# State space part in pairs of chunks with gram products as row tiles, and PReLU split between two engines

## The chip, the cores and the metric

One core of a Trainium2 chip runs the kernel: TensorE (matrix products, from SBUF into PSUM), VectorE, ScalarE, GpSimd, and SyncE, whose queue issues all of the kernel's DMAs. The metric is the device time of one execution in microseconds. All data are float32.

## The reference, cut to what matters

A selective state space layer (4 batches, 8 heads, 768 tokens, head size 32, state size 16), then a feed-forward block with PReLU on its 3072 rows of 256 values. The reference takes chunks of 32 tokens; the result doesn't depend on the size of a chunk.

```python
for c in range(nc):                       # chunks of tokens, state carried along
    cum = np.cumsum(log(clip(a))[chunk])
    L = np.exp(cum_i - cum_j) * causal    # decay from token j to token i
    M = einsum('bhin,bhjn->bhij', C, B) * L
    y = einsum('bhij,bhjd->bhid', M, x) + einsum('bhin,bhnd->bhid', C, state) * exp(cum)
    state = exp(sum(la)) * state + sum_j(B_j x_j * exp(cum_last - cum_j))
h = y_as_rows @ w_in                      # (3072, 256) by (256, 2048)
g = np.maximum(h, 0) + alpha * np.minimum(h, 0)
out = g @ w_out                           # (2048, 256)
```

## The kernel before

Chunks have Q = 128 tokens, so there are 24, six to a batch. Per batch, `batch_prep` brings B and C into layout with (head, state) on partitions by transposes on TensorE (`transposed`, L186, copied out at L190 on ScalarE and L192 on VectorE), scans a into running products `pf` (forward, L207) and `pr` (backward, L209), and makes `cd` = C times `pf`, `br` = B times `pr`, and `bn`, which is `br` transposed back.

Per chunk, `chunk` does the following. GpSimd clamps `abc`, a copy of a on all partitions (L239). VectorE scans it into the decay matrices `dec` of the eight heads (L243). ScalarE makes `cz`, eight copies of C in each of which only one head's rows are kept (L249). TensorE multiplies `bh` with four heads of `cz` at a time, 512 columns and all 128 rows of the array (`gram`, L254); VectorE multiplies by `dec` (`m`, L256). TensorE adds the part of the state (L262) and the eight products of `m` and `xt` (L267), as tiles of 32 columns of the array, into `y`; ScalarE copies `y` into `xT` (L273). The next state is `dps` (L278), masked to the blocks of the heads (L281, L284), plus the decayed old one (L285).

The second part takes groups of four chunks, 512 tokens. `hidden` makes 16 tiles `hp` of 128 x 512 (L299), each by two products; PReLU is two operations of VectorE, `neg` = min(hp, 0) * alpha (L302) and `gt` = max(hp, 0) + neg (L304). `output` multiplies `gt` with `w_out` (`po`, L315), copies to `o_sb` (L317) and stores. In the trace each float32 product is two instructions of TensorE.

The weights come as float64 and are made float32 by seven operations of VectorE and one of GpSimd for each of 32 pieces (L141 to L154): those of `w_in` after the first chunks, those of `w_out` during the first group. The code of a group emits, for each of four quarters, one chunk of the next group and then four tiles of `hidden`; `output` follows. The Tile framework orders each engine's instructions from that by priority and readiness as it models them; on the chip each engine runs its own in the order so fixed. PSUM has eight banks: two for `gram`, one for `y`, one for all other products of the state space part (`sm`), two for `hp`, two for `po`.

Of the kernel before, what the change touches and what calls it, by code (L numbers as in the profile page):

```python
# [18 lines left out]
def kernel(  # L19
# [27 lines left out]
    HD = H * D  # L47
    d_model, d_ff = moe_w_in.shape
# [4 lines left out]
    NG = NCH // GC  # L53
    FQ = 4
# [5 lines left out]
    ld = ctx.enter_context(tc.tile_pool(name="ld", bufs=1))  # L60
# [17 lines left out]
    loads = {}  # L78

    def load_batch(b):  # L80
        bc = ld.tile([P, 2, H, R * N], F32, name="bc")
        for i, src in enumerate((B, C)):
            nc.sync.dma_start(out=bc[:, i], in_=src[b].rearrange("h (p r) n -> p h (r n)", r=R))
        ahn = ld.tile([P, S], F32, name="ahn")
        for h in range(H):
            row = a[b, h : h + 1, :]
            nc.sync.dma_start(
                out=ahn[h * N : (h + 1) * N, :],
                in_=bass.AP(tensor=row.tensor, offset=row.offset, ap=[[0, N], [1, S]]),
            )  # L90
        loads["b", b] = bc, ahn

    def load_chunk(gc):
        b, c = divmod(gc, CPB)
        sl = slice(c * Q, (c + 1) * Q)
        first = a[b, 0:1, sl]
        abc = lda.tile([P, H * Q], F32, name="abc")
        nc.sync.dma_start(
            out=abc.rearrange("p (h t) -> p h t", h=H),
            in_=bass.AP(tensor=first.tensor, offset=first.offset, ap=[[0, P], [S, H], [1, Q]]),  # L100
        )
        xt = ldx.tile([P, HD], F32, name="xt")
        nc.sync.dma_start(
            out=xt.rearrange("p (h d) -> p h d", h=H), in_=x[b, :, sl, :].rearrange("h p d -> p h d")
        )
        loads["c", gc] = abc, xt

    load_batch(0)
    for gc in range(2):
        load_chunk(gc)  # L110
# [28 lines left out]
        # the upper word without its sign orders as a float32: hold it to the  # L139
        # words whose exponent float32 has, with its zero and its infinity  # L140
# [41 lines left out]
    def transposed(dst, src, eng):  # L182
        for r0 in range(0, R, 3):
            ps = ps_s.tile([P, 512], F32, name="sm")
            for r in range(3):
                nc.tensor.transpose(ps[:, r * P : (r + 1) * P], src(r0 + r), ident)  # L186
            o = dst(r0)
            i = ps[:, : 3 * P].rearrange("q (r p) -> q r p", r=3)
            if eng == "act":
                nc.scalar.copy(out=o, in_=i)  # L190
            else:
                nc.vector.tensor_copy(out=o, in_=i)  # L192

    def batch_prep(b):
        """B and C with (h n) on partitions; the running product of a from each
        chunk's start up to a token (pf), and from after it to the chunk's end (pr)."""
        bc, ahn = loads.pop(("b", b))
        d0 = prep.tile([P, S + 1], F32, name="d0")
        d1 = prep.tile([P, S], F32, name="d1")
        nc.vector.tensor_scalar(out=d0[:, :S], in0=ahn, scalar1=1e-6, scalar2=1.0,  # L200
                                op0=ALU.max, op1=ALU.min)
        nc.gpsimd.memset(d1, 0.0)
        nc.vector.tensor_copy(out=d1[:, ::Q], in_=d0[:, 0:S:Q])
        nc.vector.memset(d0[:, ::Q], 0.0)
        pf = bat.tile([P, S], F32, name="pf")
        pr = prep.tile([P, S], F32, name="pr")
        nc.vector.tensor_tensor_scan(out=pf, data0=d0[:, :S], data1=d1, initial=0.0,  # L207
                                     op0=ALU.mult, op1=ALU.add)
        nc.vector.tensor_tensor_scan(out=pr[:, ::-1], data0=d0[:, 1:][:, ::-1],  # L209
                                     data1=ends[:, ::-1], initial=0.0,  # L210
                                     op0=ALU.mult, op1=ALU.add)

        bh = bat.tile([P, S], F32, name="bh")
        ch = bat.tile([P, S], F32, name="ch")
        for i, t, eng in ((0, bh, "act"), (1, ch, "dve")):
            # token p * R + r of the batch is row p of piece r
            src = bc[:, i].rearrange("p h (r n) -> p r h n", r=R)
            nat = prep.tile([P, R, H * N], F32, name="nat")
            nc.scalar.copy(out=nat.rearrange("p r (h n) -> p r h n", h=H), in_=src)
            tv = t.rearrange("q (p r) -> q r p", r=R)  # L220
            transposed(lambda r0: tv[:, r0 : r0 + 3], lambda r: nat[:, r], eng)
        cd = bat.tile([P, S], F32, name="cd")
        nc.vector.tensor_tensor(out=cd, in0=ch, in1=pf, op=ALU.mult)
        br = prep.tile([P, S], F32, name="br")
        nc.vector.tensor_tensor(out=br, in0=bh, in1=pr, op=ALU.mult)
        bn = bat.tile([P, CPB, P], F32, name="bn")
        transposed(lambda r0: bn[:, r0 : r0 + 3], lambda c: br[:, c * Q : (c + 1) * Q], "act")
        pre[b] = pf, bh, ch, cd, bn

    def chunk(gc):  # L230
        b, c = divmod(gc, CPB)
        if c == 0:
            batch_prep(b)
        pf, bh, ch, cd, bn = pre[b]
        abc, xt = loads.pop(("c", gc))
        sl = slice(c * Q, (c + 1) * Q)
# [4 lines left out]
        nc.gpsimd.memset(abc[:, ::Q], 0.0)  # L241
        dec = work.tile([P, H, Q], F32, name="dec")
        nc.vector.tensor_tensor_scan(out=dec.rearrange("p h t -> p (h t)"), data0=abc,  # L243
                                     data1=ident_h, initial=0.0, op0=ALU.mult, op1=ALU.add)

        # C with all rows but a head's own cleared, head by head
        cz = work.tile([P, H, Q], F32, name="cz")
        for h in range(H):
            nc.scalar.mul(cz[:, h], ch[:, sl], bm3[:, h, 0:1])  # L249
        m = work.tile([P, H, Q], F32, name="m")  # L250
# [24 lines left out]
        if c < CPB - 1:  # L275
# [6 lines left out]
            else:  # L282
# [91 lines left out]
```

## Time and profile before

| what | value |
|---|---|
| median of 3 runs | 524.29 us (523.46 to 526.51) |
| span of the profiled execution | 523.9 us |
| TensorE products busy | 453.4 us, 87% |
| VectorE busy | 340.6 us, 65% |
| ScalarE busy | 85.6 us, 16% |
| GpSimd busy | 70.9 us, 14% |
| moved by DMA | 32.31 MB |

The profiled execution's own time is known as its span, from the first to the last instruction; the runs give device times. Busy times are unions over the span and say nothing yet of which engine set the end in which stage.

### The profile page before, as it was taken

The numbers are of one execution on the slowest core, as the hardware profiler recorded it, in microseconds if no ns is written. First come the engines' busy times: TensorE is split into PE (matmuls) and PEld (weight loads), VectorE is DVE, ScalarE is ACT, GpSimd is POOL, SyncE is SP. The second block draws the span as 40 slices with busy tenths as digits, with TensorE's granted clock in tenths as the row PEclk, the third lists the DMA queues.
The fourth block names the chain that finished last, engine by engine and source line by source line (L and its number), as shares of the span: only waits on it lengthen the run. The fifth ranks groups of instructions, "written<-read, shape, count | busy, mean of one in ns | idle before, by whom it ended". The sixth has DMA issues, their size and how long they took to land. (4 is left out here: it accounts for less than half of the span.)

```text
span 523.9 us, 4981 instructions
## 1 busy us (share of the span) xinstructions
PE 453.4 (87%) x1825; PEld 270.0 (52%) x1825; DVE 340.6 (65%) x587; ACT 85.6 (16%) x249; POOL 70.9 (14%) x93
## 2 busy tenths in 40 slices
PE   0285656595989999998999999998999999999997
PEld 0142222352447644685434786443884447863586
DVE  3889999999898599403899404879107964038600
ACT  2174220006220010001732000054002200000000
POOL 3413443222324000000010000102000000000000
PEclk9997967987999999999899999999999999999999
DMA  8734646323225012102222102204000000000000
GB/s 188 198 103 131 154 127 175 111 72 98 53 67 137 27 50 60 41 21 60 55 68 61 39 21 62 60 0 102 0 20 22 0 1 0 21 20 0 1 20 20
DMA packets 67192, 32.31 MB, mean 62 GB/s; under 512 B 34896, under 2 KB 62560, under 8 KB 67168
## 3 DMA queue, kind: packets, MB, share of 16 engines
q1 hardware_dynamic: 67168, 32.00, 23.0%
q8 instruction: 14, 0.23, 0.2%
q14 instruction: 10, 0.08, 0.0%
HBM read 28.84 MB, written 3.15 MB: 61 GB/s over the span
## 5 line engine op out<-in xcount | busy, mean ns | idle before, releaser
L299 PE MATMUL hp<-xT,w_in 128*128 128x512 f32 x384 | 186.4, 625 | 12.0 <-DVE gt L304 11.9
L315 PE MATMUL po<-w_out,gt 128*128 128x256 f32 x768 | 169.4, 380 | 3.8 <-POOL abc L241 2.7
L315 PEld LDWEIGHTS po<-w_out,gt 128*128 128x128 f32 x768 | 145.3, 190 | 30.7 <-issue 5.8
L299 PEld LDWEIGHTS hp<-xT,w_in 128*128 128x128 f32 x384 | 70.3, 197 | 97.5 <-issue 57.3
L317 DVE COPY o_sb<-po 128x256 f32<-128x256 f32 x24 | 10.1, 422 | 130.5 <-PE po L315 130.4
L302 DVE TENSOR_SCALAR neg<-hp,alpha 128x512 f32<-128x512 f32 x96 | 71.5, 746 | 25.1 <-PE hp L299 24.9
L249 ACT ACTIVATE cz<-ch,bmask 128x128 f32<-128x128 f32 x192 | 59.3, 390 | 99.3 <-PE gram L254 85.5
L304 DVE SCALAR_TENSOR_TENSOR gt<-hp,neg 128x512 f32<-128x512 f32 x96 | 66.0, 689 | 2.4
L239 POOL TENSOR_SCALAR abc<-abc 128x1024 f32<-128x1024 f32 x24 | 35.7, 1488 | 223.4 <-DMA abc<-in_a_dram 196.9
L243 DVE TENSOR_TENSOR_SCAN dec<-abc,ident_h 128x1024 f32<-128x1024 f32 x24 | 55.3, 2304 | 1.9 <-POOL abc L241 1.4
L254 PE MATMUL gram<-cz,bh 128*128 128x512 f32 x96 | 54.2, 669 | 1.3 <-ACT cz L249 1.2
L273 ACT COPY xT<-y 128x256 f32<-128x256 f32 x24 | 8.9, 372 | 160.9 <-PE y L267 160.8
L256 DVE TENSOR_TENSOR m<-gram,dec 128x512 f32<-128x512 f32 x48 | 31.9, 682 | 4.7 <-PE gram L254 4.6
L267 PE MATMUL y<-m,xt 128*32 128x128 f32 x384 | 21.4, 301 | 12.7 <-DVE m L256 12.7
L267 PEld LDWEIGHTS y<-m,xt 128*32 128x32 f32 x384 | 8.2, 112 | 39.0 <-DVE m L256 20.7
L254 PEld LDWEIGHTS gram<-cz,bh 128*128 128x128 f32 x96 | 18.0, 206 | 18.0 <-issue 12.5
L186 PE MATMUL sm<-ident,nat 128*128 128x128 f32 x48 | 11.1, 353 | 12.6 <-DVE alpha L175 3.9
L154 POOL TENSOR_TENSOR w_out<-wr,wt 128x256 uint32<-128x256 uint32 x16 | 15.4, 960 | 34.0 <-DVE wr L150 22.6
L186 PEld LDWEIGHTS sm<-ident,nat 128*128 128x128 f32 x48 | 6.6, 172 | 21.6 <-DVE ch L192 5.3
L262 PEld LDWEIGHTS y<-cd,state 128*128 128x128 f32 x80 | 12.3, 198 | 9.5 <-issue 8.5
L190 ACT COPY bh<-sm 128x384 f32<-128x384 f32 x8 | 6.8, 845 | 61.0 <-PE sm L186 61.0
L154 POOL TENSOR_TENSOR w_in<-wr,wt 128x256 uint32<-128x256 uint32 x16 | 12.7, 797 | 28.9 <-DVE wr L150 28.7
(43 smaller groups left out, 200.0 us busy)
## 6 DMA issues: line engine op xcount, KB each, us to landing
abc<-in_a_dram SPq DMA_DIRECT2D x24, 512.0 KB, 4.0
raw<-in_moe_w_in_dram SPq DMA_DIRECT2D x16, 256.0 KB, 2.9
raw<-in_moe_w_out_dram SPq DMA_DIRECT2D x16, 256.0 KB, 2.7
xt<-in_x_dram SPq DMA_DIRECT2D x24, 128.0 KB, 2.7
out_dram<-o_sb SPq DMA_DIRECT2D x12, 256.0 KB, 2.1
bc<-in_B_dram SPq DMA_DIRECT2D x4, 384.0 KB, 3.6
bc<-in_C_dram SPq DMA_DIRECT2D x4, 384.0 KB, 4.9
ahn<-in_a_dram SPq DMA_DIRECT2D x32, 48.0 KB, 3.1
```

Of the source, the lines that this page charges most:

```text
L154: nc.gpsimd.tensor_tensor(out=d, in0=r, in1=t, op=ALU.add)
L186: nc.tensor.transpose(ps[:, r * P : (r + 1) * P], src(r0 + r), ident)
L239: nc.gpsimd.tensor_scalar(out=abc, in0=abc, scalar1=1.0, scalar2=1e-6, op0=ALU.min, op1=ALU.max)
L243: nc.vector.tensor_tensor_scan(out=dec.rearrange("p h t -> p (h t)"), data0=abc, data1=ident_h, initial=0.0, op0=ALU.mult, op1=ALU.add)
L249: nc.scalar.mul(cz[:, h], ch[:, sl], bm3[:, h, 0:1])
L254: nc.tensor.matmul(gram.rearrange("p h t -> p (h t)"), bh[:, sl], cz[:, hs].rearrange("p h t -> p (h t)"), start=True, stop=True)
L256: nc.vector.tensor_tensor(out=m[:, hs], in0=gram, in1=dec[:, hs], op=ALU.mult)
L267: nc.tensor.matmul(y[32 * k : 32 * k + 32, w], xt[:, h * D : (h + 1) * D], m[:, h], start=(c == 0 and w == 0), stop=True, tile_position=(0 ...
L299: nc.tensor.matmul(hp, w_in[:, k, f * P : (f + 1) * P], xts[g][:, k], start=(k == 0), stop=(k == KC - 1))
L302: nc.vector.tensor_scalar(out=neg, in0=hp, scalar1=0.0, scalar2=alpha[:, f : f + 1], op0=ALU.min, op1=ALU.mult)
L304: nc.vector.scalar_tensor_tensor(out=gt[:, j], in0=hp, scalar=0.0, in1=neg, op0=ALU.max, op1=ALU.add)
L315: nc.tensor.matmul(po[:, :d_model], gts[g, f // FQ][:, f % FQ, ts], w_out[:, f], start=(f == 0), stop=(f == NF - 1))
```

## The change

The state space part runs in pairs of chunks, 12 in all. B and C are loaded per pair in their natural layout (`nat`: tokens on partitions), in rows of 16 values, and transposed per pair (four transposes, `tp`). `bn` is no longer transposed back: GpSimd multiplies the natural B by the backward running product, which is made from 96 rows (batch, head, chunk) twice in the run (`rows_prep`) and transposed. `cz` becomes two masked copies of C, even and odd heads (mask `par`), and `gram` becomes, per chunk, four products on 32 rows of the array each (two heads, 256 columns), into four PSUM banks. `m` is then made in four operations per pair. The masked product `dm` and the copy into `xT` are made for both chunks at once. The pools `ps_g` and `ps_y` go; all state space products share four banks (`ss`). The copy of a for the batch (`ahn`) is one DMA. PReLU becomes relu(hp) and relu(-hp) on ScalarE and one operation of VectorE, relu(hp) - alpha * relu(-hp). Comments are also taken out.

```diff
-    ps_g = ...(name="ps_g", bufs=2)   # also ps_y bufs=1, ps_s bufs=1
+    ps_s = ...(name="ps_s", bufs=4)
+    def load_pair(gp):
+        b, c = divmod(2 * gp, CPB)
+        nat = ldx.tile([P, 2, 2, H * N], F32, name="nat")
+        abc = lda.tile([P, 2, H * Q], F32, name="abc")
+        xt = ldx.tile([P, 2, HD], F32, name="xt")
+        for k in range(2):
+            sl = slice((c + k) * Q, (c + k + 1) * Q)
+            for i, src in enumerate((B, C)):
+                nc.sync.dma_start(out=nat[:, i, k].rearrange("p (h n) -> p h n", h=H),
+                                  in_=src[b, :, sl, :].rearrange("h p n -> p h n"))
...
+    def rows_prep(i):
+        rows = loads.pop(("r", i))
+        d0 = prep.tile([RW, Q + 1], F32, name="r0")
+        nc.vector.tensor_scalar(out=d0[:, :Q], in0=rows, scalar1=1e-6, scalar2=1.0,
+                                op0=ALU.max, op1=ALU.min)
...
+        nc.vector.tensor_tensor_scan(out=pr[:, ::-1], data0=d0[:, 1:][:, ::-1],
+                                     data1=ends[:RW, ::-1], initial=0.0,
+                                     op0=ALU.mult, op1=ALU.add)
+        ps = ps_s.tile([P, 512], F32, name="ss")
+        nc.tensor.transpose(ps[:, :RW], pr, ident[:RW, :RW])
...
+        for k in range(2):
+            nc.vector.tensor_tensor_scan(out=dec[:, k].rearrange("p h t -> p (h t)"),
+                                         data0=abc[:, k], data1=ident_h, initial=0.0,
+                                         op0=ALU.mult, op1=ALU.add)
+        tp = ps_s.tile([P, 512], F32, name="ss")
+        for i in range(2):
+            for k in range(2):
+                nc.tensor.transpose(tp[:, (2 * i + k) * P : (2 * i + k + 1) * P], nat[:, i, k],
+                                    ident)
+        ct = tp[:, 2 * P :]
+        bh = work.tile([P, 2, Q], F32, name="bh")
+        nc.scalar.copy(out=bh.rearrange("p k t -> p (k t)"), in_=tp[:, : 2 * P])
+        cz = work.tile([P, 2, 2, Q], F32, name="cz")
+        for e in range(2):
+            nc.scalar.mul(cz[:, e].rearrange("p k t -> p (k t)"), ct, par[:, e : e + 1])
+        cd = work.tile([P, 2, Q], F32, name="cd")
+        nc.vector.tensor_tensor(out=cd.rearrange("p k t -> p (k t)"), in0=ct,
+                                in1=pf[:, c * Q : (c + 2) * Q], op=ALU.mult)
...
-        for h in range(H):
-            nc.scalar.mul(cz[:, h], ch[:, sl], bm3[:, h, 0:1])
-        for g in range(2):
-            hs = slice(4 * g, 4 * g + 4)
-            gram = ps_g.tile([P, 4, Q], F32, name="gram")
-            nc.tensor.matmul(gram.rearrange("p h t -> p (h t)"), bh[:, sl],
-                             cz[:, hs].rearrange("p h t -> p (h t)"), start=True, stop=True)
-            nc.vector.tensor_tensor(out=m[:, hs], in0=gram, in1=dec[:, hs], op=ALU.mult)
+        gram = [ps_s.tile([P, 2, 2 * Q], F32, name="ss") for r in range(4)]
+        for k in range(2):
+            for r in range(4):
+                rs = slice(32 * r, 32 * r + 32)
+                nc.tensor.matmul(gram[r][:, k], bh[rs, k], cz[rs, :, k], start=True, stop=True,
+                                 tile_position=(32 * r, 0), skip_group_check=True)
+        for r in range(4):
+            hs = slice(2 * r, 2 * r + 2)
+            nc.vector.tensor_tensor(out=m[:, :, hs].rearrange("p k h t -> p k (h t)"), in0=gram[r],
+                                    in1=dec[:, :, hs].rearrange("p k h t -> p k (h t)"),
+                                    op=ALU.mult)
...
             neg = op.tile([P, GT], F32, name="neg")
-            nc.vector.tensor_scalar(out=neg, in0=hp, scalar1=0.0, scalar2=alpha[:, f : f + 1],
-                                    op0=ALU.min, op1=ALU.mult)
-            nc.vector.scalar_tensor_tensor(out=gt[:, j], in0=hp, scalar=0.0, in1=neg,
-                                           op0=ALU.max, op1=ALU.add)
+            nc.scalar.activation(out=gt[:, j], in_=hp, func=ACTF.Relu)
+            nc.scalar.activation(out=neg, in_=hp, func=ACTF.Relu, scale=-1.0)
+            nc.vector.scalar_tensor_tensor(out=gt[:, j], in0=neg, scalar=nalpha[:, f : f + 1],
+                                           in1=gt[:, j], op0=ALU.mult, op1=ALU.add)
...
-            if g + 1 < NG:
-                ssm((g + 1) * GC + q)
+            if g + 1 < NG and q % 2 == 0:
+                ssm((g + 1) * GC // 2 + q // 2)
```

The pair's order in the code is: clamp and `dec`, transposes, `bh`, `cz`, `cd`, then `bn`, `dps`, `dm` and the states, then `gram` and `m`, then all of `y`, then the copy into `xT`. The loads of a pair are issued one pair ahead.

## Rows read from the trace of the kernel before

**Rows 1.** The page, busy time of each engine.
```profile
PE 453.4 (87%) x1825; PEld 270.0 (52%) x1825; DVE 340.6 (65%) x587; ACT 85.6 (16%) x249; POOL 70.9 (14%) x93
```
**Rows 2.** Windows: length, busy PE, PEld, DVE, ACT, POOL; clock; DMA share, GB/s.
```profile
0.00:19.20 19.20, 0.26 (x1) 0.18 (x1) 10.24 (x10) 3.71 (x10) 6.97 (x15) 1.00 0.77 182
19.20:161.30 142.10, 101.14 (x391) 49.79 (x392) 134.43 (x313) 37.90 (x109) 46.30 (x50) 0.86 0.41 112
161.30:520.30 359.00, 351.99 (x1435) 220.07 (x1434) 195.54 (x267) 43.98 (x130) 17.66 (x29) 1.00 0.13 35
```
**Rows 3.** Waits of PE, 161.3 to 520.3 us: total, times, longest.
```profile
PE hp L299 <- DVE gt L304: 3.9, 5, 1.2
PE sm L186 <- DVE ch L192: 2.3, 2, 2.0
PE y L267 <- DVE m L256: 0.4, 1, 0.4
```
**Rows 4.** The chain that ended last: start, us, what, instructions.
```profile
341.03 0.34 PE sm L186 x3
...
405.29 1.72 PE gram L254 x4
407.00 0.44 PE y L262 x4
...
407.88 0.36 PE y L267 x8
408.24 1.05 PE hp L299 x2
...
429.77 0.57 PE y L267 x16
...
436.67 27.63 PE po L315 x128
464.30 28.31 PE hp L299 x64
```
**Rows 5.** Groups of DVE by shape, 0 to 161.3 us: busy us, mean ns.
```profile
L243 DVE TENSOR_TENSOR_SCAN dec<-abc,ident_h 128x1024 f32<-128x1024 f32 x10 | 23.3, 2331 | 1.0 <-POOL abc L241 1.0
...
L302 DVE TENSOR_SCALAR neg<-hp,alpha 128x512 f32<-128x512 f32 x16 | 11.8, 740 | 2.5 <-PE hp L299 2.5
L304 DVE SCALAR_TENSOR_TENSOR gt<-hp,neg 128x512 f32<-128x512 f32 x16 | 10.8, 680 | 0.0
...
L209 DVE TENSOR_TENSOR_SCAN pr<-d,ends 128x768 f32<-128x768 f32 x2 | 4.3, 2172 | 0.0
...
L192 DVE COPY ch<-sm 128x384 f32<-128x384 f32 x4 | 3.3, 834 | 0.4 <-PE sm L186 0.4
...
L223 DVE TENSOR_TENSOR cd<-ch,pf 128x768 f32<-128x768 f32 x2 | 2.4, 1180 | 0.0
L225 DVE TENSOR_TENSOR br<-bh,pr 128x768 f32<-128x768 f32 x2 | 1.9, 952 | 0.7 <-ACT bh L190 0.7
```
**Rows 6.** Groups of ACT by shape, whole span.
```profile
L249 ACT ACTIVATE cz<-ch,bmask 128x128 f32<-128x128 f32 x192 | 59.3, 390 | 99.3 <-PE gram L254 85.5 <-DVE ch L192 13.8
...
L273 ACT COPY xT<-y 128x256 f32<-128x256 f32 x24 | 8.9, 372 | 160.9 <-PE y L267 160.8
...
L190 ACT COPY bh<-sm 128x384 f32<-128x384 f32 x8 | 6.8, 845 | 61.0 <-PE sm L186 61.0
...
L190 ACT COPY bn<-sm 128x384 f32<-128x384 f32 x8 | 3.8, 474 | 4.5 <-PE sm L186 4.4
```
**Rows 7.** Timeline of the first stage: start, us, instruction, idle before it.
```profile
11.16 2.60 DVE L209 TENSOR_TENSOR_SCAN pr<-d,ends 128x768 f32<-128x768 f32 x1
...
66.11 0.43 PE L267 MATMUL y<-m,xt 128*32 128x128 f32 x8 [2.12 <-DVE m L256]
```
**Rows 8.** Groups of PE by shape, 161.3 to 520.3 us: gram.
```profile
L254 PE MATMUL gram<-cz,bh 128*128 128x512 f32 x60 | 29.0, 597 | 0.0
```
**Rows 9.** DMA queues: packets, MB, share of 16 engines' span.
```profile
q1 hardware_dynamic: 67168, 32.00, 23.0%
```

More of the change, by code (lines that the diff above doesn't have):

```diff
@@ L47 @@
     HD = H * D
+    RW = batch // 2 * H * CPB
     d_model, d_ff = moe_w_in.shape
@@ L53 @@
     NG = NCH // GC
+    NP = NCH // 2
     FQ = 4
@@ new lines, in load_batch, with load_rows @@
+        loads["b", b] = ahn
+    def load_rows(i):
+        rows = ld.tile([RW, Q], F32, name="rows")
+        nc.sync.dma_start(out=rows, in_=a.rearrange("b h (c t) -> (b h c) t", t=Q)[i * RW : (i + 1) * RW])
+        loads["r", i] = rows
+    def load_pair(gp):
[8 more added lines that the diff above has]
+                                  in_=src[b, :, sl, :].rearrange("h p n -> p h n"))
+            first = a[b, 0:1, sl]
@@ L87, in load_batch @@
             nc.sync.dma_start(
-                out=ahn[h * N : (h + 1) * N, :],
-                in_=bass.AP(tensor=row.tensor, offset=row.offset, ap=[[0, N], [1, S]]),
-            )
[L91 to L106, printed above, removed]
+                out=abc[:, k].rearrange("p (h t) -> p h t", h=H),
@@ L108 @@
+                in_=bass.AP(tensor=first.tensor, offset=first.offset, ap=[[0, P], [S, H], [1, Q]]),
+            )
+            nc.sync.dma_start(out=xt[:, k].rearrange("p (h d) -> p h d", h=H),
+                              in_=x[b, :, sl, :].rearrange("h p d -> p h d"))
+        loads["p", gp] = nat, abc, xt
+    load_rows(0)
     load_batch(0)
-    for gc in range(2):
-        load_chunk(gc)
+    load_pair(0)
     w_in = const.tile([P, KC, d_ff], F32, name="w_in")
@@ L180 @@
     state = {}
[L182 to L192, printed above, removed]
+    prt = {}
@@ L213, in batch_prep @@
[L213 to L231, printed above, removed]
+        pre[b] = pf
+    def pair(gp):
+        b, c = divmod(2 * gp, CPB)
@@ L232, in chunk @@
         if c == 0:
             batch_prep(b)
-        pf, bh, ch, cd, bn = pre[b]
-        abc, xt = loads.pop(("c", gc))
-        sl = slice(c * Q, (c + 1) * Q)
+        pf = pre[b]
+        nat, abc, xt = loads.pop(("p", gp))
+        last = c + 2 == CPB
         nc.gpsimd.tensor_scalar(out=abc, in0=abc, scalar1=1.0, scalar2=1e-6,
                                 op0=ALU.min, op1=ALU.max)
[L241 to L244, printed above, removed]
@@ new lines, in pair @@
+        bn = work.tile([P, 2, H * N], F32, name="bn")
+        i, bi = divmod(b, 2)
+        pj = prt[i].rearrange("p (b h c) -> p b c h", b=2, h=H)[:, bi, c : c + 2]
+        nc.gpsimd.tensor_tensor(
+            out=bn.rearrange("p k (h n) -> p k h n", h=H),
+            in0=nat[:, 0].rearrange("p k (h n) -> p k h n", h=H),
+            in1=pj.unsqueeze(3).to_broadcast([P, 2, H, N]), op=ALU.mult)
+        nk = 1 if last else 2
+        dps = ps_s.tile([P, 512], F32, name="ss")
+        for k in range(nk):
+            nc.tensor.matmul(dps[:, k * HD : (k + 1) * HD], bn[:, k], xt[:, k], start=True, stop=True)
@@ new lines, in pair @@
+        dm = work.tile([P, 2, HD], F32, name="dm")
+        nc.vector.tensor_tensor(
+            out=dm[:, :nk], in0=dps[:, : nk * HD].rearrange("p (k m) -> p k m", m=HD),
+            in1=bmask.unsqueeze(1).to_broadcast([P, nk, HD]), op=ALU.mult)
+        st = [state.get(b)]
+        for k in range(nk):
+            if st[k] is None:
+                st.append(dm[:, k])
+                continue
+            new = work.tile([P, HD], F32, name=f"state{k}")
+            e = (c + k + 1) * Q - 1
+            nc.vector.scalar_tensor_tensor(out=new, in0=st[k], scalar=pf[:, e : e + 1],
+                                           in1=dm[:, k], op0=ALU.mult, op1=ALU.add)
+            st.append(new)
@@ L331, in weights @@
             load_weights(*p)
-    for i in range(GC):
+    for i in range(GC // 2):
         ssm(i)
-        weights(in_pieces, i, GC)
+        weights(in_pieces, i, GC // 2)
     for g in range(NG):
```

116 lines of the change are left out of this document (59 added, 57 removed).

## The prediction

> **What bounds the kernel now.** I read the busy line of the page first [rows 1]: TensorE is busy 87% of 523.9 us, VectorE 65%, ScalarE 16%. An average hides the stages, so next came the windows [rows 2]. The reader is to see two regimes in them. From 19.2 to 161.3 us VectorE is busy 134.4 of 142.1 us and TensorE only 101.1, partly at a granted clock of 0.86: VectorE sets the pace. It turns the weights into float32 there, and does the scans and the PReLU of the first group. From 161.3 to 520.3 us TensorE is busy 352.0 of 359.0 us at a clock of 1.00, VectorE 195.5: TensorE sets the pace. The waits of TensorE in that second stretch add to 6.6 us, of which 3.9 are for gt (L304) and 2.3 for ch (L192) [rows 3]. The chain of waits from 400 us on is TensorE nearly alone, and gives the rates [rows 4]: 64 instructions of hp, the 16 tiles of a group, in 28.31 us, 1.77 us a tile; four instructions of gram, one chunk, in 1.72 us.
>
> So the change has two places where it can pay: work taken off VectorE before 161.3, and work taken off TensorE behind it. VectorE work saved behind 161.3 pays only through the waits of rows 3; TensorE work saved before 161.3 I count at nothing.
>
> **PReLU.** Removed: neg on VectorE (L302), 0.740 us x 16 = 11.8 us before 161.3 [rows 5]. The operation that stays has both inputs in SBUF; L304 has one of its two in PSUM and takes 0.680 [rows 5], and I take the same. Added: two relus of 128x512 from PSUM per tile on ScalarE. The trace has copies from PSUM of 256 elements in 372 ns and of 384 in 474 ns, so 128 elements more cost 102 ns; 512 come to 576 ns, a tile to 1.15 us [rows 6]. That is inside TensorE's 1.77 us, and hp is given back earlier than now, after 1.15 us against 0.74 + 0.68 = 1.42 us. With 2 us per pair for the copies of bh, cz and xT on the same queue (below), ScalarE has 16 x 1.15 + 2 x 2 = 22.4 us in a hidden phase in which TensorE has 28.3 us of hp and two pairs. It does not bind, so I cost the relus at nothing; cover is TensorE's hp work.
>
> **Batch preparation.** Gone from VectorE per batch: the reverse scan (2.17 us), two copies of ch (0.834 each), br (0.952) [rows 5]; 4.8 us x the two batches that are prepared before 161.3 = 9.6. cd moves from 1.18 us per batch to one 128x256 product per pair, of a third of the elements, 0.4 us: 2.4 us [rows 5] against 4.5 pairs x 0.4 = 1.8, gain 0.6. rows_prep adds a clamp, a scan of 128 and a small copy, some 1.1 us. The reverse scan of batch 0 runs at 11.16 us [rows 7], where VectorE is busy only 10.2 of the first 19.2 us for want of loads [rows 2], so its 2.2 us give nothing. dec, m, dm and state keep their elements, only grouped by pairs: nothing.
> VectorE stretch: 11.8 + 9.6 + 0.6 - 1.1 - 2.2 = **18.7 us**, if the stretch stays VectorE's own. Its bounds are 0 (something else takes over) and 21.
>
> **Gram as four row tiles.** Now: 8 instructions of 512 columns per pair, 2 x 1.72 = 3.44 us [rows 4]. After: 2 chunks x 4 tiles x 2 instructions = 16 of 256 columns. A 256-column instruction takes 27.63 / 128 = 0.216 us by itself [rows 4]. No row shows row tiles. The nearest are y's column tiles: a run of 8 holds TensorE for 0.36 us, a run of 16 for 0.57 [rows 4]. So 8 more cost 0.21 us, and a run's switch in and out some 0.15. A full-array instruction of 128 columns takes 0.11 us (four of L262 in 0.44); eight alone would need 0.88, hence tiles run four at a time. If row tiles do too, 16 instructions are 4 slots of 0.216 = 0.86, with 0.15 for the switch and 0.1 for the first load 1.11 us. Bounds: one after another, 16 x 0.216 + 0.15 = 3.6 us (nothing gained); and between them, paced by loading the stationary operand: each tile loads 128 columns, where y's tiles load 32, and three transposes, each with a 128-column load, take 0.34 us, 0.113 each [rows 4]; 16 x 0.113 + 0.25 = 2.06 us. I take 1.11, since the only tiles in the trace run side by side. Behind 161.3 lie 60 gram instructions, 15 chunks, 7.5 pairs [rows 8]: 7.5 x 2.33 = **17.5 us**; 10.4 at 2.06; -1.2 at 3.6.
>
> **The rest on TensorE.** y's tiles of a pair can form one run of 32: 4 x 0.21 + 0.15 = 1.0 us against 4 x 0.36 = 1.44. The run may be cut by hp, as it is now by two hp instructions [rows 4], so I take 0.3 a pair, **2.2 us**. Transposes behind 161.3 fall from 36, 18 in each of two batches, to 30 and a small one: **0.6 us**. The waits for gt and ch, 6.2 us, lose their cause; the new order transposes, bh and cz on ScalarE, gram, four products m on VectorE, y must be filled with hp. Its own latency is 0.46 + 2 x 0.49 on ScalarE (a cz of 256 elements: 390 ns for 128 [rows 6] + 102) and 4 x 0.68 on VectorE, 4.2 us, against 28 us of hp per group to put between. Today's chain, gram then m then y, is filled with hp and waits 0.4 us in all [rows 3]. I leave 3 us for it: **3.2 us** net.
>
> **Loads.** B and C come as 48 transfers of 1024 rows of 64 bytes in place of eight of 1024 rows of 384: 41,000 packets more. The mean packet now takes 0.230 x 16 x 523.9 / 67,168 = 28.7 ns of an engine [rows 9], so 73 us of all sixteen over the run. Behind 161.3 the queues are 13% busy [rows 2]: nothing. Before it, 5 of 12 pairs add 31 us to 0.41 x 142 = 58 us in a stretch that would shrink to some 123: 89 of 123, hidden, but no longer by much. The first pair waits for some 2.0 MB where now 2.5 MB (B and C of a whole batch, a, two chunks) come first. I cost the loads at nothing; without cover see the fourth rival.
>
> **Sum.** 18.7 + 17.5 + 2.2 + 0.6 + 3.2 = 42.2 us. The profiled execution spans 523.9 us, the median of the runs is 524.29, so what lies around the span is inside their scatter (523.46 to 526.51). 523.9 - 42.2 = **482 us**.
>
> **Rivals.**
> Row tiles don't run side by side, or are paced by their loads. For it: y's tiles load 32 columns, these 128. Against: nothing in the trace. Loads: 482 + 7.1 = 489 us. One after another: 482 + 18.7 = 501 us. In the second form that part of the change doesn't do what it says.
> The pair's chain stalls the in-order TensorE. For it: without hp to put between, TensorE waited 2.12 us for m at 66.11 [rows 7]. At 2 us a pair beyond the 3 us allowed, 7.5 x 2 = 15 more: 497 us. This is also the case that ends **slower**: if nothing fills the chain and dec (2 x 2.33 us [rows 5]) stands before m as well, a pair loses 4.2 + 4.7 = 8.9 us, 7.5 x 8.9 = 67 less the 3 allowed: 546 us. It turns slower from (526.5 - 479) / 7.5 = 6.3 us a pair. Against: after 161.3 TensorE found hp to do in nearly every such gap.
> ScalarE becomes the bound. For it: its strided copy of 384 elements took 845 ns [rows 6]; at that rate 512 take 1.13, a tile 2.25 us. A hidden phase would have 16 x 2.25 + 4 = 40 us of ScalarE against 28.3 + 2 x 4.5 = 37 on TensorE (a pair by the rates above: 1.1 gram, 1.0 and 0.9 y, 0.9 dps, 0.5 transposes), 3 us in each of four groups, and 16 x (2.25 - 1.77) = 7.7 in the last: 502 us. Against: that copy writes with a stride, relus write contiguously. The Trainium skill (ScalarE: Activation LUTs, Rules for kernel authors) speaks against the change here: it gives relu, max and min to VectorE, which it puts at up to about 3 times faster per element in bf16. In float32 the rows don't bear that out: ScalarE's 474 ns for 384 contiguous elements lie in line with VectorE's 0.680 us for 512, and ScalarE stands at 16% where VectorE is the bound. By the rule's factor on 0.680 us two relus would take an estimated 4.1 us a tile, and ScalarE would set the time of every group.
> The first stretch doesn't shorten, because loads in 64-byte rows come late: 482 + 18.7 = 501 us. For it: 89 of 123 us above. Against: each pair's loads are issued a pair ahead.
>
> **How the numbers follow.** Forecast (474 to 490): 0.52. Loads pace the tiles, 489: 0.10. Tiles one after another, 501: 0.10. Chain stalls of about 2 us, 497: 0.11. ScalarE as the bound, 502: 0.03. First stretch unchanged, 501: 0.06. Chain unfilled, slower: 0.04; half way to it, no change: 0.02. More than the sum, under 472: 0.02. The range takes in the single mishaps and a little of two together: 462 to 505. It leaves out the last two kinds and pairs of mishaps, some 0.15. The three runs lie within 0.6% of each other, so 0.5% is about what can be told from no change: faster 0.94, same 0.02, slower 0.04.
>
> **What would show each step.** VectorE: the end of the first group's hp some 19 us earlier, VectorE still near 95% busy from 20 to 140 us. PReLU: relus at 0.58 us, no hp waiting for ScalarE. Gram: the 16 instructions of a pair within 1.1 us; 2.1 us means loads, 3.6 one after another. Chain: waits of gram for cz and of y for m under 3 us in all behind the first stretch. Loads: the wait of the first scans, and of transposes for nat. The prediction is wrong above all if TensorE's waits per pair exceed 2 us, or if the first group ends no earlier.

## The result, and the profile after

The changed kernel takes 493.96 us (median of 4 runs, 492.96 to 495.49) against 524.40 us (median of 4 runs, the three of the table ahead among them); the ratio is 0.9417 (95% interval 0.939 to 0.9444). It is faster, inside the range of 462 to 505, and 12 us above the 482 that was forecast. The profiled executions span 492.1 us after and 523.9 before: 31.8 us gained where the sum had 42.2. The other 1.7 of the 12 us are not in the sum: the profiled execution of the changed kernel takes 493.78 us and spans 492.1, and the forecast took the 482 from a span, with nothing added for what lies around it. Page of after, busy time and DMA queue:

```profile
PE 427.6 (87%) x1899; PEld 276.8 (56%) x1899; DVE 274.7 (56%) x485; ACT 126.7 (26%) x249; POOL 74.0 (15%) x81
...
q1 hardware_dynamic: 108512, 32.10, 28.4%
```

Against [rows 1, 9], VectorE lost 66 us and ScalarE gained 41, and there are 41,344 more packets for the same bytes. To see where the gain arose, both traces are cut at the same two events: where the last input of the first group's `po` is ready, and where TensorE comes to the last of that group's `po`. In the kernel before the last input is a `gt` of VectorE, at 158.2; in the changed kernel it is the last addition into `w_out`, on GpSimd, at 148.1. Windows of after (length; busy PE, PEld, DVE, ACT, POOL; clock; DMA share, GB/s):

```profile
0.00:19.20 19.20, 3.04 (x10) 2.23 (x10) 6.27 (x15) 4.09 (x12) 5.77 (x14) 1.00 0.76 150
19.20:148.10 128.90, 90.34 (x366) 50.75 (x364) 122.22 (x283) 24.30 (x48) 49.77 (x48) 0.79 0.63 140
148.10:164.30 16.20, 16.15 (x74) 13.89 (x74) 16.06 (x18) 0.00 (x0) 4.89 (x4) 1.00 0.49 147
164.30:488.50 324.20, 318.06 (x1453) 209.96 (x1451) 129.74 (x172) 98.34 (x189) 13.52 (x16) 1.00 0.12 27
```

Windows of the kernel before, cut at the same two events:

```profile
19.20:158.20 139.00, 98.04 (x368) 48.13 (x368) 131.33 (x310) 37.52 (x108) 43.20 (x50) 0.85 0.42 114
158.20:174.90 16.70, 16.70 (x88) 13.63 (x87) 10.01 (x11) 0.37 (x1) 7.12 (x7) 1.00 0.42 111
174.90:520.30 345.40, 338.38 (x1372) 208.10 (x1370) 188.63 (x259) 43.98 (x130) 13.64 (x22) 1.00 0.12 31
```

The reader is to see that the two regimes stayed. VectorE is busy 95% of the second window in both kernels, and the stretch ends at 148.1 instead of 158.2: 10.1 us where 18.7 were forecast. VectorE itself has done its last operation for the first group at 145.3. The last addition on GpSimd, fed by it, takes 2.64 us, where 23 of the 32 take 0.72 to 0.73; it starts 0.16 us into a `dec` scan of VectorE and ends 0.5 us after it, and TensorE waits for it (start, us, instruction, idle before it):

```profile
145.41 2.64 POOL L160 TENSOR_TENSOR w_out<-wr,wt 128x256 uint32<-128x256 uint32 x1 [2.50 <-DVE wr L156]
...
148.11 16.55 PE L353 MATMUL po<-w_out,gt 128*128 128x256 f32 x74 [2.10 <-POOL w_out L160]
```

The `po` left over takes 16 to 17 us in both. Behind it TensorE is busy 98% in both, and this stretch, to the end of the span, is 327.8 us instead of 349.0: 21.2 us where the terms 17.5, 2.2, 0.6 and 3.2 made 23.5. With the 10.6 us of the first stretch that is the whole 31.8.

Groups of VectorE up to 148.1 us, and of ScalarE over the span (busy us, mean ns of one):

```profile
L244 DVE TENSOR_TENSOR_SCAN dec<-abc,ident_h 128x1024 f32<-128x1024 f32 x10 | 24.0, 2419 | 1.0 <-POOL abc L241 1.0
...
L342 DVE SCALAR_TENSOR_TENSOR gt<-neg,nalpha,gt 128x512 f32<-128x512 f32 x16 | 16.4, 1031 | 1.9 <-ACT neg L341 1.7
...
L340 ACT ACTIVATE gt<-hp 128x512 f32<-128x512 f32 x96 | 57.3, 597 | 123.2 <-PE hp L337 123.2
...
L341 ACT ACTIVATE neg<-hp 128x512 f32<-128x512 f32 x96 | 56.8, 592 | 13.5 <-DVE gt L342 13.5
```

The relus cost what was forecast (0.597 and 0.592 us against 0.576). `gt` did not: 1.031 us in the first stretch, against 0.680 in [rows 5]. The 80 behind 164.3 us, where GpSimd has little to do (ns, shortest, median, longest; first and last start):

```profile
L342 DVE SCALAR_TENSOR_TENSOR gt<-neg,nalpha,gt x80: 723/751/1891, 172.7 to 462.0; 128x512 f32<-128x512 f32 x80
```

The timeline shows why, and how a pair runs (start, us, instruction, idle before it):

```profile
15.38 0.17 DVE L187 TENSOR_SCALAR nalpha<-ss 128x16 f32<-128x16 f32 x1 [5.49 <-PE ss L186]
...
17.01 4.88 DVE L244 TENSOR_TENSOR_SCAN dec<-abc,ident_h 128x1024 f32<-128x1024 f32 x2 [1.02 <-POOL abc L241]
...
25.93 0.28 DVE L147 TENSOR_SCALAR wt<-raw 128x256 uint32<-128x256 uint32 x1
...
92.14 0.73 POOL L160 TENSOR_TENSOR w_out<-wr,wt 128x256 uint32<-128x256 uint32 x1 [2.04 <-DVE wr L156]
...
92.19 1.23 DVE L342 SCALAR_TENSOR_TENSOR gt<-neg,nalpha,gt 128x512 f32<-128x512 f32 x1
...
164.58 1.15 PE L299 MATMUL ss<-cz,bh 32*128 32x256 f32 x16
166.49 1.16 PE L312 MATMUL ss<-cd,state 128*128 128x128 f32 x8 [0.76 <-DVE m L303]
167.58 0.63 PE L319 MATMUL ss<-m,xt 128*32 128x128 f32 x12
168.14 1.12 PE L337 MATMUL hp<-xT,w_in 128*128 128x512 f32 x2
169.20 0.85 PE L319 MATMUL ss<-m,xt 128*32 128x128 f32 x20
```

A `gt` that starts while GpSimd does its addition takes 1.23 us, against a median of 0.751. Of the 16 in the first stretch ten start while an addition is under way and take 1.02 to 1.24 us; the other six take 0.74 to 0.75. And the 16 instructions of `gram` run in 1.15 us, as forecast, but 0.76 us of waiting for `m` follows, and `y` is cut in two by `hp`.

That pair is the fastest of eight: the other seven take 1.38 to 1.98 us. In each of them one row tile starts late, 0.05 to 0.06 us after VectorE has finished the `cd` or `dm` that reads one of the four `ss` banks. In the pair below it starts at 301.49, when `cd` has ended at 301.43:

```profile
300.87 1.74 PE L299 MATMUL ss<-cz,bh 32*128 32x256 f32 x16
...
301.02 0.41 DVE L262 TENSOR_TENSOR cd<-ss,pf 128x256 f32<-128x256 f32 x1
```

The wait for `m` is the only one that the waits of TensorE hold from 164.3 to 488.5 us (total, times, longest):

```profile
PE ss L312 <- DVE m L303: 5.9, 8, 1.9
```

The chain that ended last shows a later pair from VectorE's side, and the rate of `hp` at the end:

```profile
369.17 0.68 DVE m L303
369.85 0.04 issue
369.89 1.16 PE ss L312 x8
371.05 0.56 PE ss L319 x12
371.61 1.06 PE hp L337 x2
372.67 0.78 PE ss L319 x20
...
433.35 27.47 PE hp L337 x64
```

To split the second stretch, the time from the start of each TensorE instruction to the start of the next is summed by what the instruction makes; I call these sums slots. A wait falls to the slot before it.

| slots behind the first group's `po`, us | before | after |
|---|---|---|
| `gram`, with the wait behind it | 27.3 (15 chunks) | 18.6 (16 chunks) |
| `hp` | 151.4 (0.476 an instruction) | 140.7 (0.440) |
| `y`, the part of `m` | 10.3 | 10.3 |
| `y`, the part of the state | 6.7 | 7.8 |
| `dps` and transposes | 11.3 | 8.1 |
| `po` | 137.9 | 137.9 |

`hp`, which the sum had only in its 3.2 us of waits, gives more than `gram`.

The profiled executions of e2 and e5, below, were disturbed ones and are not read; their times come from the other executions.

### The profile page after: what moved, and what is told of

Read it like the earlier page. It is cut to its first block, busy times and chain, and to the rows that moved or that the text cites. A ratio compares the mean times of both kernels' runs of the same rounds, so it can differ in the third digit from the quotient of the medians.

```text
span 492.1 us, 5000 instructions
## 1 busy us (share of the span) xinstructions
PE 427.6 (87%) x1899; PEld 276.8 (56%) x1899; DVE 274.7 (56%) x485; ACT 126.7 (26%) x249; POOL 74.0 (15%) x81
## 4 chain that ended last, share of the span: by engine, by line
PE 58%; DVE 2%; ACT 0%; issue 0%
PE po L353 28%; PE hp L337 25%; PE ss L319 2%; PE ss L312 1%; DVE m L303 1%; PE ss L276 1%; PE ss L299 1%; PE ss L253 0%; DVE dm L278 0%; DVE state L288 0%; DVE gt L342 0%; ACT gt L340 0%; ACT neg L341 0%; DVE cd L262 0%; DVE o_sb L355 0%
## 5 line engine op out<-in xcount | busy, mean ns | idle before, releaser
L342 DVE SCALAR_TENSOR_TENSOR gt<-neg,nalpha,gt 128x512 f32<-128x512 f32 x96 | 79.4, 833 | 66.9 <-ACT neg L341 66.5
L340 ACT ACTIVATE gt<-hp 128x512 f32<-128x512 f32 x96 | 57.3, 597 | 123.2 <-PE hp L337 123.2
L355 DVE COPY o_sb<-po 128x256 f32<-128x256 f32 x24 | 10.1, 421 | 122.5 <-PE po L353 122.4
L341 ACT ACTIVATE neg<-hp 128x512 f32<-128x512 f32 x96 | 56.8, 592 | 13.5 <-DVE gt L342 13.5
L299 PE MATMUL ss<-cz,bh 32*128 32x256 f32 x192 | 32.8, 464 | 19.3 <-DVE cd L262 16.0
L299 PEld LDWEIGHTS ss<-cz,bh 32*128 32x128 f32 x192 | 20.1, 211 | 34.2 <-DVE cd L262 19.0
L239 POOL TENSOR_SCALAR abc<-abc 128x2048 f32<-128x2048 f32 x12 | 25.2, 2098 | 85.4 <-DMA abc<-in_a_dram 71.6
L303 DVE TENSOR_TENSOR m<-ss,dec 128x512 f32<-128x512 f32 x48 | 30.4, 681 | 2.2 <-PE ss L299 2.2
L269 POOL TENSOR_TENSOR bn<-nat,prt 128x256 f32<-128x256 f32 x12 | 10.6, 883 | 85.7 <-PE ss L276 52.5
L319 PE MATMUL ss<-m,xt 128*32 128x128 f32 x384 | 21.1, 310 | 1.9 <-DVE m L303 1.9
L160 POOL TENSOR_TENSOR w_out<-wr,wt 128x256 uint32<-128x256 uint32 x16 | 15.8, 985 | 43.4 <-DVE wr L156 43.4
L319 PEld LDWEIGHTS ss<-m,xt 128*32 128x32 f32 x384 | 12.1, 118 | 12.8 <-issue 6.1
L152 DVE SCALAR_TENSOR_TENSOR wr<-wt,wr 128x256 uint32<-128x256 uint32 x32 | 16.7, 521 | 0.0
```

The costliest lines, as they stand in the source:

```text
L152: nc.vector.scalar_tensor_tensor(out=r, in0=t, scalar=0x40000000, in1=r, op0=ALU.bitwise_and, op1=ALU.bitwise_or)
L160: nc.gpsimd.tensor_tensor(out=d, in0=r, in1=t, op=ALU.add)
L299: nc.tensor.matmul(gram[r][:, k], bh[rs, k], cz[rs, :, k], start=True, stop=True, tile_position=(32 * r, 0), skip_group_check=True)
L303: nc.vector.tensor_tensor(out=m[:, :, hs].rearrange("p k h t -> p k (h t)"), in0=gram[r], in1=dec[:, :, hs].rearrange("p k h t -> p k (h t)"),
L319: nc.tensor.matmul(y[32 * q : 32 * q + 32, w, k], xt[:, k, h * D : (h + 1) * D], m[:, k, h], start=False, stop=True, tile_position=(0, 32 ...
L340: nc.scalar.activation(out=gt[:, j], in_=hp, func=ACTF.Relu)
```

## Experiments

Times are medians, and ratios are to the kernel before in the same series. "First stretch" ends with the first group's last `po`.

**The two halves alone.** e1 puts only the new PReLU into the kernel before; e2 puts the old PReLU back into the changed kernel.

```diff
-nc.vector.tensor_scalar(out=neg, in0=hp, scalar1=0.0, scalar2=alpha[:, f : f + 1], ...min, mult)
-nc.vector.scalar_tensor_tensor(out=gt[:, j], in0=hp, scalar=0.0, in1=neg, ...max, add)
+nc.scalar.activation(out=gt[:, j], in_=hp, func=ACTF.Relu)
+nc.scalar.activation(out=neg, in_=hp, func=ACTF.Relu, scale=-1.0)
+nc.vector.scalar_tensor_tensor(out=gt[:, j], in0=neg, scalar=nalpha[:, f : f + 1], in1=gt[:, j], ...mult, add)
```

> The kernel before, with nothing but the new PReLU (two relus on ScalarE, one operation on VectorE with both inputs in SBUF). Theory: the operation that stays waits for GpSimd in the first stretch (1.03 us on average in the changed kernel, 0.68 before), so that stretch gains 11.8 - 5.6 = 6 us; behind it the hp slots shrink from 0.476 to 0.440 us, some 11 us: 524 - 17 = 507. Rival, PReLU pays in the first stretch alone, as predicted: 11.8 + the 4 us of waits for gt, 508 with all of it in front and hp slots unchanged. Rival, the pairs bring it all: 522 or more.

e1: 508.51 us, 0.9723 (0.9692 to 0.9754). The slots of `hp` shrink as the theory said, to 0.444 us an instruction; the first stretch gains 10.1 us, where it had 6.

> The changed kernel with the PReLU of before (two operations on VectorE). Theory: the pairs alone give what is left of 31 us, some 14: 510, with gram slots as in the changed kernel (1.2 to 2.0 us for 16 instructions) and hp slots back near 0.47 us. Rival, the pairs only pay because ScalarE took the PReLU: 520 or more. Rival, the pairs bring it all: 495.

e2: 512.50 us, 0.9783 (0.9748 to 0.9817). The same kernel was profiled again as e12.

> The pairs with the PReLU of before once more, for its profile: 511 to 513. Theory, behind the first stretch hp slots near 0.47 us as before, gram slots near 2 us a pair, and the first stretch ends about where it did before (173 to 176 us). Rival, the pairs shorten the first stretch by the 9.6 us of preparation that VectorE no longer does: it ends at 165.

e12: one time, 509.62 us, 2.9 below the median of e2. The first stretch ends at 167.1, near the rival's 165 and not at 173 to 176; the slots of `hp` are 0.458 us. Cut by stretch, in spans, the gains are: relus alone 10.1 and 7.5 us, pairs alone 7.8 and 8.2, both together 10.6 and 21.2. The halves overlap in the first stretch (7.3 us less than their sum) and help each other behind it (5.5 us more), as far as one execution of e12 shows: by the medians of e1 and e2 the halves give 14.8 and 10.8 of the 30.4 us, so together 4.8 more than apart. Waits of TensorE in e12 behind its first stretch:

```profile
PE hp L336 <- DVE gt L341: 6.6, 5, 1.6
PE ss L311 <- DVE m L302: 5.1, 8, 1.6
```

With the old PReLU, `hp` still waits for VectorE, and its slots are 146.7 us; in e1 they are 142.0, with no wait of `hp` for `gt`. So 9.4 of the 10.7 us of `hp` come with the relus alone, which give its banks back through ScalarE; the pairs alone bring 4.7.

**Are the row tiles what pays, and does their order matter?** e3 emits the products tile by tile; e7 keeps the pairs and makes `gram` with the whole array, four products of 512 columns per pair, with the eight masked copies per chunk back on ScalarE.

```diff
-for k in range(2):
-    for r in range(4):
+for r in range(4):
+    for k in range(2):
```

> The changed kernel with the two loops around the gram products exchanged: both chunks of one row tile follow each other before the next tile, same instructions, same operands. Theory, tiles run side by side only when different tiles follow each other: 16 instructions of a pair then take some 13 slots of 0.216 = 2.8 us in place of 1.0 to 2.0, 8 pairs behind the first stretch, 494 + 6 to 14 = 500 to 508. Rival, the order of tiles doesn't matter (TensorE sorts it out, or the gram products are hidden): 494 within 0.5%.

e3: 495.87 us, 0.9469 (0.9441 to 0.9498): within 0.5% of the changed kernel, and behind the first stretch the same 327.8 us. Timeline of a pair:

```profile
303.11 1.74 PE L299 MATMUL ss<-cz,bh 32*128 32x256 f32 x16
305.02 1.16 PE L312 MATMUL ss<-cd,state 128*128 128x128 f32 x8 [0.17 <-DVE m L303]
```

The products take as long as in the same pair of the changed kernel (1.74 us at 300.87). The wait behind them is shorter, and `y` longer, 14.5 us of slots against 10.3. Three tiles start 13 ns apart here (303.108, 303.121, 303.134), though three more instructions of the first tile stand ahead of the second's in the order emitted.

```diff
-nc.scalar.mul(cz[:, e].rearrange(...), ct, par[:, e : e + 1])
+nc.scalar.mul(cz[:, h], ct[:, k * Q : (k + 1) * Q], bm3[:, h, 0:1])
...
-nc.tensor.matmul(gram[r][:, k], bh[rs, k], cz[rs, :, k], ..., tile_position=(32 * r, 0), ...)
+nc.tensor.matmul(gram.rearrange("p h t -> p (h t)"), bh[:, k], czs[k][:, hs].rearrange(...), ...)
```

> The changed kernel with the gram products as before: four of 512 columns per pair on all 128 rows, and eight masked copies of C per chunk on ScalarE for it (4 us more of ScalarE per pair; one buffer of the loads less). Theory, a pair's gram then holds TensorE 3.4 us in place of 1.6 and its wait: 8 pairs, 9 to 15 us, 503 to 509. Rival, the row tiles bring nothing because m and its wait come after them anyway: 494 to 497.

e7: 497.31 us, 0.9492 (0.9456 to 0.9528), just above the rival's range and far from the theory's. Timeline of a pair:

```profile
369.65 2.11 PE L302 MATMUL ss<-cz,bh 128*128 128x512 f32 x4
371.60 1.02 PE L336 MATMUL hp<-xT,w_in 128*128 128x512 f32 x2
372.45 1.88 PE L302 MATMUL ss<-cz,bh 128*128 128x512 f32 x4
374.17 1.05 PE L311 MATMUL ss<-cd,state 128*128 128x128 f32 x8
375.16 1.08 PE L318 MATMUL ss<-m,xt 128*32 128x128 f32 x32
```

`gram` is long again, 29.1 us of slots, but `y` waits for nothing and runs in one piece (8.7 us instead of 10.3). Behind the first stretch e7 takes 333.9 us, the changed kernel 327.8: as built, row tiles are worth 6.1 us there, where the sum had 17.5, and 3 us in the whole time; e7's first stretch is 2.9 us shorter, for a cause that no run shows.

**Who slows `gt`?** e4 leaves VectorE one input in PSUM, with one relu on ScalarE (`nalpha` is minus alpha):

```diff
+nc.scalar.activation(out=neg, in_=hp, func=ACTF.Relu, scale=nalpha[:, f : f + 1])
+nc.vector.scalar_tensor_tensor(out=gt[:, j], in0=hp, scalar=0.0, in1=neg, ...max, subtract)
```

> The changed kernel with another split of PReLU: ScalarE makes relu(-alpha * hp), once, and VectorE max(hp, 0) minus it, reading hp in PSUM, so it has one input in SBUF. The same result for alpha not below zero, as here. Theory, the operation with two inputs in SBUF waits for GpSimd: this one takes 0.68 us in the first stretch beside GpSimd's additions too, the stretch ends some 5 us earlier; behind it hp is held until VectorE has read it, which may cost back part of the hp slots' gain: 485 to 494. Rival, the long operations of the first stretch come from something else: still 1.0 us there, and 494 to 500.

e4: 502.22 us, 0.9588 (0.9556 to 0.962): the expected gain did not come. Group of `gt` in the first stretch:

```profile
L341 DVE SCALAR_TENSOR_TENSOR gt<-hp,neg 128x512 f32<-128x512 f32 x16 | 10.8, 682 | 2.3 <-ACT neg L340 2.3
```

Waits of TensorE from 167.2 us on:

```profile
PE hp L337 <- DVE gt L341: 5.1, 5, 1.5
PE ss L312 <- DVE m L303: 4.1, 7, 1.6
```

So the cause of the 1.03 us is shown: with `hp` in PSUM the operation takes 0.682, and the ten that run beside an addition of GpSimd take 0.67 to 0.69. The first stretch ends only 1.6 us earlier than in the changed kernel, not 5: VectorE now runs 11 `dec` scans, some of them the next group's, ahead of its last `gt`, where 8 stood before. But VectorE reads `hp` last again, the slots of `hp` go from 140.7 to 149.9 us, and the second stretch is 9.7 us longer.

**Do the loads hold the first stretch?** e5 issues the load of alpha first and three pieces of the weights right behind the first pair's loads; e8 does the same and takes e4's PReLU for the first group alone.

```diff
+raws = [load_raw(src, c0, dst.shape[-1]) for dst, src, c0 in in_pieces[:3]]
...
+        raw = raws.pop(0) if raws else load_raw(src, c0, w)
```

> The changed kernel with two loads moved ahead: alpha before everything, and the first three pieces of the weights right behind the first pair's loads. In the changed kernel VectorE waited 5.5 us for alpha from 9.9 us on, and turned the first piece at 25.9 us (19.2 before). Theory, VectorE bounds the first stretch and lost its saving there to late loads: the first piece some 4 to 6 us earlier, the last of w_out too, 488 to 490. Rival, the stretch's end hangs on something else (the order of po, ScalarE): 493 to 495.

e5: 496.56 us, 0.9482 (0.9451 to 0.9514), no gain. The trace of e8 has to tell why.

> The loads of e5 together with the one-relu PReLU of e4 in the first group alone, where GpSimd is busy with the weights; the other groups keep two relus. Theory: e5's gain and some 2 to 5 us for the operation that no longer waits for GpSimd, nothing lost behind: 484 to 488. Rival, both only shift the wait for w_out: as e5.

e8: 499.36 us, 0.9536 (0.951 to 0.9563). Timeline of its VectorE:

```profile
17.58 0.69 DVE L284 TENSOR_TENSOR dm<-ss,bmask 128x512 f32<-128x512 f32 x1 [6.86 <-PE ss L282]
...
23.30 0.67 DVE L153 TENSOR_SCALAR wt<-raw 128x256 uint32<-128x256 uint32 x1
```

The first conversion starts at 23.3 instead of 25.9 us, but VectorE now waits 6.86 us for the first pair's `dps`, for which TensorE had waited 2.37 us for the load of `xt`; that the weights displaced this load is likely and not shown. VectorE finishes the first group's `gt` at 151.2. In the first stretch e8 differs from e4 by the loads alone, and it ends 4.7 us later (167.5 against 162.7). The theory that earlier weights give back what was missing falls.

**Is the first stretch VectorE's?** e6 leaves out three of VectorE's seven conversion operations for `w_out`; e10 moves `cd`, for which `gram` waited 16 us in the first stretch, to GpSimd.

```diff
-nc.vector.tensor_single_scalar(out=t, in_=hi, scalar=0x7FFFFFFF, op=ALU.bitwise_and)
-nc.vector.tensor_scalar(out=tf, in0=tf, scalar1=F64_INF, scalar2=F64_ZERO, ...)
...
-nc.vector.scalar_tensor_tensor(out=r, in0=t, scalar=0x40000000, in1=r, ...)
```

> The changed kernel without three of the seven operations of VectorE on each piece of w_out (the sign mask, the clamp and the exponent's top bit; the values of w_out are then not the reference's). That takes 16 x 1.0 us off VectorE. Theory, the last piece of w_out, that is VectorE, sets the end of the first stretch: it ends 10 to 16 us earlier, 478 to 484. Rival, TensorE at its slow clock or the PReLU bounds it: 490 to 494.

e6: 490.13 us, 0.9358 (0.9329 to 0.9386), the lower end of the rival's range. `w_out` is ready 12 us earlier, but then the last `gt` sets the event, at 139.4 and so 8.7 us earlier, with 8.2 us less of VectorE's work before it, not 16; the stretch ends 6.0 us earlier. The rest of the 8.7 is lost on TensorE. From 134 to 136 us it was busy 0.6 of 2.0 us; from 138 to 143 its granted clock is 0.50, the lower of its two levels, and the first ten `po` products take 2.2 us more than at 0.216 us each. Four more than in the changed kernel are left, another 0.9 us. Timeline and window:

```profile
139.51 19.20 PE L355 MATMUL po<-w_out,gt 128*128 128x256 f32 x78 [1.12 <-DVE gt L344]
...
139.50:142.00 2.50, 2.49 (x6) 2.05 (x7) 2.50 (x3) 0.00 (x0) 0.00 (x0) 0.50 0.79 229
```

So VectorE's work sets most of the stretch's end, and TensorE's clock part of the rest.

```diff
-nc.scalar.copy(out=bh.rearrange("p k t -> p (k t)"), in_=tp[:, : 2 * P])
+nc.scalar.copy(out=bc.rearrange("p i k t -> p (i k t)"), in_=tp)
+ct = bc[:, 1].rearrange("p k t -> p (k t)")
-nc.vector.tensor_tensor(out=cd.rearrange("p k t -> p (k t)"), in0=ct, ...)
+nc.gpsimd.tensor_tensor(out=cd.rearrange("p k t -> p (k t)"), in0=ct, ...)
```

> The changed kernel with the transposes copied out whole by ScalarE and cd made by GpSimd from the copy, so that gram's banks don't wait for VectorE's cd (one buffer of the loads less). In the changed kernel TensorE stood 16 us in the first stretch before gram for cd. Theory, TensorE's order is part of what holds the first stretch: it ends 3 to 6 us earlier, 488 to 491. Rival, the stretch is VectorE's alone and TensorE's waits there cost nothing: 493 to 495.

e10: 496.59 us, 0.9469 (0.9448 to 0.949). The 16 us wait is gone, 8.5 us of waiting for `dm` stand in its place, and the stretch ends 0.8 us earlier. So TensorE's waits there are, at least mostly, VectorE's lateness under another name. The time lies above both expectations: behind the first stretch e10 takes 330.7 us and not 327.8, with 9.9 us of waits for `m` where 5.9 were.

**Does the order around `y` eat the row tiles' gain?** e9 emits `y` and its copy (`then`) behind the quarter's four tiles of `hp`; e11 adds e10.

```diff
-ssm((g + 1) * GC // 2 + q // 2)
+then = ssm((g + 1) * GC // 2 + q // 2)
 hidden(g, q)
+then()
```

> The changed kernel with one change of order: the products into y and the copy into xT of a pair are emitted behind the quarter's four hp tiles, so that seven hp products stand on TensorE between gram and y where none stood. Theory, what the row tiles save is eaten by the wait for m behind them (5.9 us over 8 pairs after the first stretch) and by y's run cut by hp: both go, 6 to 9 us, 485 to 489. Rival, the row tiles are slow in themselves: the gram slots stay at 2 us a pair and the time at 492 to 494.

e9: 484.56 us, 0.9245 (0.9219 to 0.927). It beats both kernels. Timeline of a pair:

```profile
363.31 1.45 PE L299 MATMUL ss<-cz,bh 32*128 32x256 f32 x16
364.69 6.28 PE L340 MATMUL hp<-xT,w_in 128*128 128x512 f32 x14
370.80 1.05 PE L315 MATMUL ss<-cd,state 128*128 128x128 f32 x8
371.79 1.08 PE L322 MATMUL ss<-m,xt 128*32 128x128 f32 x32
```

Waits of TensorE behind the first stretch:

```profile
PE hp L340 <- ACT neg L344: 0.4, 1, 0.4
```

The slots of `gram` fall from 18.6 to 12.2 us and those of `y` from 10.3 to 8.1; the second stretch is 318.2 us, 9.6 shorter; the first ends 2.0 us later.

> Both of the two edits before. If they add: 480 to 485. If the first stretch doesn't answer to TensorE: as the y edit alone, 485 to 489.

e11: 484.98 us, 0.9234 (0.9203 to 0.9265): as e9, so `cd`'s place brings nothing that the time shows. But it shows the row tiles without a wait for a bank: six of the seven whole runs of `gram` behind the first stretch take 1.15 us, and a pair's slots 1.08. Timeline:

```profile
362.90 1.15 PE L300 MATMUL ss<-cz,bh 32*128 32x256 f32 x16
```

## Why the direction was right and the size 12 us off

**The two regimes** were read rightly, and so were the two places where the change pays. The terms were not.

**VectorE's stretch, 18.7, measured 10.1.** The step that failed is "L304 has one of its two in PSUM and takes 0.680, and I take the same": 16 x (1.031 - 0.680) = 5.6 us. The sentence named the difference between the operations and then priced it at nothing. The Trainium skill (SBUF — State Buffer, Who interferes with whom) has the rule: a VectorE instruction with two SBUF inputs contends with a GpSimd instruction that reads SBUF, one with at most one such input, outside the modes that use both ports, does not. The runs agree: 1.23 us beside GpSimd's addition, 0.75 without, 0.682 in e4. The rest: the 18.7 are 20.9 us of work less 2.2 of idling. Up to its last operation for the first group VectorE works 125.7 us, before 141.5, so 15.8 us less; that is 5.1 short, the 5.6 of `gt` less some small gains. It idles 19.6 us, before 16.6: 3.0 where 2.2 were written off. The place is the start: in the first 19.2 us VectorE does 6.3 us of work where it did 10.2 [rows 2], and the first conversion of a weight now stands behind a whole pair's work, at 25.9 us. And the forecast had no term for GpSimd's last addition, which ends 2.7 us behind VectorE. 18.7 - 5.1 - 0.8 - 2.7 = 10.1.

**`gram`, 17.5, measured 8.7 in slots (with one chunk more) and 6.1 by e7.** The tiles run four at a time, and 1.11 us a pair was near the 1.15 of the pairs that find their banks free. What failed is the PSUM around them, two waits that the forecast did not price. `gram` takes all four `ss` banks. In seven of eight pairs VectorE still reads one of them, for `cd` or `dm`, and the tile of that bank starts late; e11, with `cd` off VectorE, shows the runs without it. And `y` stands right behind `gram` in the queue and needs one of the four banks, so it waits for the first `m`, 5.9 us in eight pairs, where the forecast allowed 3 for all such waits. In the kernel before, `y` had a bank of its own, and its part of the state stood between `gram` and `m`'s product [rows 4]; the forecast counted on `hp` there. The rival "the chain stalls" was right in kind, at 0.74 us a pair and not 2. e9 shows the second cause by taking it away.

**`y`, 2.2, measured nothing.** The run stayed cut by two `hp` instructions, and the part of the state takes 1.1 us more, with one chunk more in it. In e9 and e7, uncut, `y` gains 2.2 and 1.6 us.

**Waits, 3.2, measured 10.7 in the slots of `hp`.** That the relus release `hp` earlier stands in the forecast; it was priced by the waits of [rows 3] alone. The slots show that the waits listed were the smaller part of what VectorE cost `hp`. e1 has most of the gain without pairs, e4 loses nearly all of it. Here the forecast was too low, and that hid most of what `gram` fell short by. That the second stretch came out near its terms, 21.2 us against 23.5, is luck.

**Transposes, 0.6, measured 1.6**; `dps`, which the sum did not have, gives as much again.

**Rivals.** Tiles one after another, or paced by their loads: false, 16 instructions in 1.15 us against 3.6 and 2.06; the longer runs hold a wait for a bank. ScalarE as the bound: false; TensorE has no wait for a relu behind the first stretch, so the preference of the Trainium skill for VectorE (ScalarE: Activation LUTs, Rules for kernel authors) did not decide here. The first stretch held by loads in small rows: it shortened all the same, by 10.6 us, and moving the weights up did not help (e5, e8); what the small rows cost is not shown.

**Open.** Why the halves overlap in the first stretch was not settled. Alone, each has a `gt` as the last input, at 148.5 (e1) and 151.6 us (e12); together VectorE is done at 145.3, and GpSimd's late addition takes back 2.7 us of that. That the scan beside it is what holds this addition is likely by its times, and no run tested it.

## What to carry to other kernels

When an operation moves, check where its neighbour's inputs now lie: a VectorE operation that loses its PSUM input may have to share a way into SBUF with GpSimd. A shorter product on an in-order TensorE pays only if the next instruction in the queue is ready: look at what stands behind it, which PSUM banks both need and who still reads them, and put independent products between, which here was worth 9 us more. Who reads a PSUM bank last sets the pace of the products that fill it, and the list of waits understates it; sum the time from start to start.

## What the hardware showed unexpectedly

Emitted tile by tile, row tiles still start together: in e3 the first instructions of three tiles start 13 ns apart, though each tile's own second starts only 0.32 us after its first (303.428). The Trainium skill (TensorE: Matmul & The Clock Gate, The mechanism, under What overlaps and what doesn't) says that products are not reordered; by the starts in this trace, instructions of another row tile passed waiting ones of a busy tile, and the order of emission cost nothing measurable. That the queue held them tile by tile is inferred from pairs in which the fourth tile waits for its bank: in e3 the first tile's third instruction, of the second chunk, runs before it (236.471 against 236.790 us), in the changed kernel only behind it (234.797 against 234.790).

`gt` takes 0.75 us from SBUF without GpSimd and 0.682 with one input in PSUM: the slower form for `gt` is the one that frees PSUM, and the kernel as a whole is faster with it, 493.96 us against 502.22.
